# The down products of a step in two parts, with the token group between them

## The chip, the cores and the metric

The kernel runs on one core of a Trainium2 chip. The time is the device time of one execution in microseconds (us); lower is better. Three runs of the kernel before are given, and one more execution was profiled.

## What is computed

Eight sequences of 3008 tokens with 256 channels are Fourier transformed along the sequence, mixed in the frequency domain by a complex 256x256 matrix, soft thresholded, transformed back, and every token then goes through a feed-forward net of 256 -> 2048 -> 256.

```python
def _attn_ref(x, w_r, w_i, b_r, b_i):
    X = np.fft.rfft(x, axis=1)                      # x: (8, 3008, 256)
    Xr, Xi = X.real, X.imag
    Yr = Xr @ w_r - Xi @ w_i + b_r
    Yi = Xr @ w_i + Xi @ w_r + b_i
    Yr = np.sign(Yr) * np.maximum(np.abs(Yr) - 0.01, 0.0)
    Yi = np.sign(Yi) * np.maximum(np.abs(Yi) - 0.01, 0.0)
    return np.fft.irfft(Yr + 1j * Yi, n=3008, axis=1)

def _moe_ref(x, w_in, w_out):                       # x: (24064, 256)
    h = x @ w_in                                    # w_in: (256, 2048)
    g = h * (1.0 / (1.0 + np.exp(-1.702 * h)))
    return g @ w_out                                # w_out: (2048, 256)
```

## The kernel before

3008 is 64 x 47, so the transform is done in two stages, of length 47 and of length 64, each a set of matmuls. All large products are made of three matmuls (`mm3`): weights and data are each split into a rounded high part and a rest, and high x high, high x rest and rest x high are added up in PSUM.

The main loop has 47 x 8 = 376 steps. Tile `k` of the feed-forward net is 512 tokens; step `q` of a tile does 256 of the 2048 hidden channels. A step issues, in the program's order:

- `cur.up(q)`: 12 matmuls of 512 columns (`pa<-th` and `pa<-tl`) into two PSUM banks, each read out by ScalarE with the gated activation (`gb`, L684). From `gb` ScalarE and VectorE make the right factors of the down product: three blocks (`hb`, `lb`) and four sums and differences of blocks (`ht`, `lt`), since the down product is a 2x2 block product with seven multiplications.
- pieces of the spectral work of the next batch (`spectral`): the 64-point stage (`pa<-kr,br`), the mixing (`pa<-wf_h,zz` and `pa<-wf_..,zz`, read out by VectorE as `mv`), the inverse (`pa<-yh,ki`). A list of steps with costs spreads them over the loop.
- `tokens_to(need)`: if the tokens that the coming steps need are not there, the next token group, `tokens(u)`: 376 tokens, about one group in six steps, 64 in all. The first two go another way (`first_tokens`).
- `behind[0].down(behind[1])`: the down products of the step before, 7 right factors x 3 = 21 matmuls of 256 columns into the four output banks `po0` to `po3` (`po<-hb`, `po<-lb`, `po<-ht`, `po<-lt`). `ORDER` gives the seven (left factor, right factor, bank, half): right factors 0, 1, 2, 3, 4, 5, 6, of which 0 to 2 are `hb` and 3 to 6 are `ht`. The fourth is the first that uses `ht`, and it goes to bank 1. Tile 0 is "plain": 4 products of 512 columns.
- After the last step of a tile, `combine()`: two copies of ScalarE (L778, L779) and additions of VectorE and GpSimd read the output banks, and two DMAs on SyncE store the result. `up` of the second step of a tile is queued behind the last down product of the tile before (`after("down")`), and the first down products of the new tile behind that `up` (`after("up")`).

PSUM has eight banks: four for the outputs, and four (`ps_a`, tile name `pa`) that `up`, the spectral stages and the token groups share. A token group writes two of these (64 matmuls `pa<-kz,ur`, the inverse stage of length 47, split into `th` and `tl` by ScalarE and VectorE). In the 40 groups of `u` = 8 to 47 it also does the forward stage of length 47 ("step 47") of a later batch: 8 matmuls `pa<-xt,kp` into two further banks, copied out by ScalarE (`aev`, L495) and stored by SyncE. It also issues the loads of later groups (`ur`, `xt`), all on SyncE's queue.

A *claim* is a matmul of 2 columns (`pa<-wi_h`) into a fresh bank. It takes the wait for that bank, so that the small matmuls behind it have none.

The order of instructions on each engine is planned by the framework's scheduler when the program is built: it goes by the program's order as priority, by what is ready in its own plan, and gives a bank when it is planned free. Where a matmul is not ready, one from further on in the program is issued. Two things tie its hands: inside `with quarters():` TensorE's instructions keep the order in which they are written (others may be issued between them), and `with after(key):` queues the instructions of the block behind the named one on its engine, without waiting for its end.

Of the kernel before, what the change touches and what calls it, by code (L numbers as in the profile page):

```python
# [19 lines left out]
S, N1, N2 = 3008, 64, 47  # L20
# [4 lines left out]
JP = 4 * 2 * N2  # L25
NU = NJ // 4
TOK, HT = 512, 256
NQ = DFF // 256
# [88 lines left out]
def fourier_mix_then_gated_ffn(ctx: ExitStack, tc: tile.TileContext, x, w_r, w_i, b_r, b_i, w_in, w_out, pack, kbs, out):  # L117
    nc = tc.nc
    NB = x.shape[0]
# [13 lines left out]
    def bank():  # L133
        return ps_a.tile([128, 512], F32, name="pa", tag="pa")
# [4 lines left out]
    def buf2(name):  # L139
        return buf([128, 2, D], F32, name, tag="w2", bufs=W2)  # L140

    def after(*keys):
        held = ExitStack()
        for k in keys:
            held.enter_context(tc.issue_after(done_at[k]))
        return held

    def split(hi, lo, src):
        nc.scalar.copy(hi, src)  # L149
        return nc.vector.tensor_tensor(lo, src, hi.bitcast(F32), ALU.subtract)  # L150

    last = [None]

    def mm(ps, w, t, start=True, stop=True):
        last[0] = nc.tensor.matmul(ps, lhsT=w, rhs=t, start=start, stop=stop).ins  # L155

    def mm3(ps, wh, wl, xh, xl, start=True, stop=True):
        mm(ps, wh, xh, start, False)
        mm(ps, wh, xl, False, False)
        mm(ps, wl, xh, False, stop)  # L160
# [16 lines left out]
    parts, done_at = {}, {}  # L177
# [66 lines left out]
    wo_h, wo_l = ([cst.tile([128, NQ // 2, 7, 128], F32R, name=f"wo_{i}a")] * (NQ // 2) for i in range(2))  # L244
# [108 lines left out]
    def quarters():  # L353
        return tc.manual_schedule(engines={mybir.EngineType.PE})

    def claim(ps):

        mm(ps[0:2, 0:2], wi_h[:, 0, 0:2], wi_h[:, 0, 0:2])
# [128 lines left out]
    def dft47_products(ps, t):  # L487
        for c, p in ((1, 1), (0, 0), (0, 1), (1, 0)):
            mm(ps[p][64 * c:64 * c + 64], kp[64 * p:64 * p + 48], t[c][64 * p:64 * p + 48])

    def dft47_out(b, n, ps):
        s1w = s1s[b].rearrange("c f p n j d -> (c f) p n (j d)")
        for p in range(2):
            ev = buf2("aev").rearrange("p j d -> p (j d)")
            nc.scalar.copy(ev, ps[p])  # L495
            nc.sync.dma_start(s1w[:, p, n], ev)
# [101 lines left out]
    def first_tokens(u):  # L598
        t = us.pop(u)
        for c in range(2):  # L600
            ps = bank()
            for j in range(4):
                mm(ps[:, 94 * j:94 * j + 94], t[:96, j, 128 * c:128 * c + 128], kzz)
            for k in range(JP * u // TOK, (JP * (u + 1) - 1) // TOK + 1):
                if k not in ytiles:
                    ytiles[k] = (fbuf([128, 2, TOK], F32R, "th"), fbuf([128, 2, TOK], F32R, "tl"))
                a = JP * u - TOK * k
                n0, n1 = max(0, -a), min(JP, TOK - a)
                split(*(t2[:, c, a + n0:a + n1] for t2 in ytiles[k]), ps[:, n0:n1])
# [11 lines left out]
    def tokens(u):  # L621
        if u < 2:
            return first_tokens(u)
        t = us.pop(u)
        step = steps47.pop(u, None)
        if step:
            b, n, _ = step
            p47 = [bank() for p in range(2)]
        ps = [bank() for p in range(2)]
        pv = [b[:, :JP].rearrange("p (c j n) -> p c j n", c=2, j=4) for b in ps]  # L630
        with quarters():
            for x47 in p47 + ps if step else ps[:1]:
                claim(x47)
            if step:
                dft47_products(p47, step[2])
            for j in range(4):
                for c in range(4):
                    i = 64 * (c % 2)
                    for p in reversed(range(2)):
                        hs = slice(64 * p, 64 * p + 48)  # L640
                        mm(pv[p][i:i + 64, c // 2, j], t[hs, j, 64 * c:64 * c + 64], kz[hs])
        if step:
            dft47_out(b, n, p47)
        for k in range(JP * u // TOK, (JP * (u + 1) - 1) // TOK + 1):
            if k not in ytiles:
                ytiles[k] = (fbuf([128, 2, TOK], F32R, "th"), fbuf([128, 2, TOK], F32R, "tl"))
            th, tl = ytiles[k]
            at = [JP * u + 94 * j - TOK * k for j in range(4)]
            js = [j for j in range(4) if 0 <= at[j] and at[j] + 94 <= TOK]
            for p in range(2):  # L650
                if js:
                    hi, lo = (t[:, :, at[js[0]]:at[js[0]] + 94 * len(js)].rearrange("p c (j n) -> p c j n", j=len(js))[:, :, :, 47 * p:47 * p + 47]
                              for t in (th, tl))
                    split(hi, lo, pv[p][:, :, js[0]:js[0] + len(js)])
                for j in range(4):
                    a = at[j] + 47 * p
                    n0, n1 = max(0, -a), min(47, TOK - a)
                    if j not in js and n0 < n1:
                        split(th[:, :, a + n0:a + n1], tl[:, :, a + n0:a + n1], pv[p][:, :, j, n0:n1])

    def fbuf(shape, dt, name, bufs=2):
        return ff.tile(shape, dt, name=name, tag=name, bufs=bufs)


    ORDER = ((0, 0, 0, 0), (1, 1, 0, 1), (3, 2, 2, 1), (4, 3, 1, 1), (6, 4, 2, 0), (5, 5, 1, 0), (2, 6, 3, 0))
    FIRST, LAST = {0: 0, 2: 2, 1: 3, 3: 6}, {0: 1, 2: 4, 1: 5, 3: 6}

    class Ffn:
        def __init__(self, k):
# [49 lines left out]
            done_at["l"] = split(ht, lt, gt).ins  # L719
            self.g[q] = [(hb[:, i], lb[:, i]) for i in range(3)] + [(ht[:, i], lt[:, i]) for i in range(4)]  # L720

        def down(self, q):
            if q == 0:
                self.acc = [ps_o.tile([128, 2, HT], F32, name=f"po{i}", tag=f"po{i}") for i in range(3 if self.plain else 4)]
            g = self.g.pop(q)
            if self.plain:

                for a, i, bk, first, final in ((0, 0, 0, True, True), (1, 1, 1, True, True), (6, 0, 2, True, False), (2, 1, 2, False, True)):
                    mm3(self.acc[bk], wo_h[q][:, q % 4, a], wo_l[q][:, q % 4, a], *g[i], start=q == 0 and first, stop=q == NQ - 1 and final)
                if q == NQ - 1:  # L730
                    o = [buf2(f"o{i}") for i in range(3)]
                    nc.scalar.copy(o[2], self.acc[0])
                    for e in range(2):
                        nc.vector.tensor_tensor(o[e], self.acc[1 + e], o[2], ALU.add)
                        nc.sync.dma_start(out[self.k, :, e], o[e].rearrange("p h n -> p (h n)"))
                return
            for n, (a, t, bk, h) in enumerate(ORDER):
                mm3(self.acc[bk][:, h], wo_h[q][:, q % 4, a], wo_l[q][:, q % 4, a], *g[t],
                    start=q == 0 and FIRST[bk] == n, stop=q == NQ - 1 and LAST[bk] == n)
            done_at["down"] = last[0]  # L740
            if q == NQ - 1:
                self.combine()
# [52 lines left out]
    done = 0  # L795
# [119 lines left out]
    queue, nextb, behind = [], 1, None  # L915
    for n in range(NT * NQ):
        k, q = divmod(n, NQ)
        if q == 0:
            cur = Ffn(k)
        with after("down") if q == 1 and k > 1 else ExitStack():  # L920
            cur.up(q)
        if n < NQ:
            if n < 7:
                with after("h", "l"):
                    weights(9 + n)
            if n:
                do_early(n)
            if n == 6:
                with after("h", "l"):
                    rounded_parts(pk)  # L930
                ahead = spectral(1, new_s2(1))
                ahead.pop(0)[1]()
            if n == 3:
                pk = packs_in()
        elif not queue and nextb < NB and (nextb < 3 or done >= NU * (nextb - 1)):
            queue = ahead if nextb == 1 else spectral(nextb, new_s2(nextb))
            total, spent, n0 = sum(c for c, _ in queue), 0.0, n
            n1 = NQ * S * nextb // TOK - 16
            nextb += 1
        while queue and spent < total * (n + 1 - n0) / (n1 - n0):  # L940
            c, step = queue.pop(0)
            spent += c
            step()
        need = TOK * (1 + (n + 2) / NQ)
        while queue and need + JP > S * (nextb - 1):
            queue.pop(0)[1]()
        if JP * done < need:
            tokens_to(need)
        if behind is not None:
            with after("up") if q == 1 and k > 1 else ExitStack():  # L950
                behind[0].down(behind[1])
        behind = (cur, q)
    behind[0].down_last(behind[1])

# [34 lines left out]
```

## Time and profile before

| | us |
|---|---|
| median of 3 runs | 2561.44 |
| lowest and highest | 2560.91, 2562.35 |
| profiled execution, first to last instruction | 2562.7 |
| TensorE busy in it | 2542.8 |
| VectorE busy in it | 1931.8 |
| ScalarE busy in it | 1608.2 |

The span of the profiled execution is the time that the profile accounts for; the runs were timed without a profile. The granted clock of TensorE was 0.999 of full speed (2.4 GHz) over the whole run, so its matmuls do not differ in clock.

### The profile page before, as it was taken

How to read it: one execution, taken by the hardware profiler on the slowest of the kernel's cores; microseconds unless marked ns; L12 is line 12 of the kernel's file. 1: busy time of each engine (PE TensorE's matmuls, PEld its weight loads, DVE VectorE, ACT ScalarE, POOL GpSimd, SP SyncE). 2: the span in 40 equal slices, each digit the busy share in tenths (PEclk: the TensorE clock that was granted, in tenths of full speed). 3: DMA queues.
4: the chain of work that ended last, by engine and by line, in shares of the span. 5: the costliest groups of instructions: out<-in, count | busy, mean ns of one | idle time of the engine just before them, and what ended most of it. 6: DMA issues, size and time to landing. Idle time of an engine off the chain costs nothing.

```text
span 2562.7 us, 49527 instructions
## 1 busy us (share of the span) xinstructions
PE 2542.8 (99%) x19979; PEld 2260.5 (88%) x19979; DVE 1931.8 (75%) x3245; ACT 1608.2 (63%) x2627; POOL 50.9 (2%) x65
## 2 busy tenths in 40 slices
PE   9999999999999999999999999999999999999999
PEld 7679999888898888998888988998989999888888
DVE  6788877777777777777777777778767777777776
ACT  4566666666666666666666666666666666665655
POOL 0000000000000000000000000000000000000000
PEclk9999999999999999999999999999999999999999
DMA  8753322333323323233233232332332132200000
GB/s 221 220 161 90 95 87 83 97 90 96 92 72 93 98 89 95 68 96 108 77 95 88 81 106 82 86 91 84 98 100 61 54 89 57 60 30 22 20 13 18
DMA packets 163623, 221.84 MB, mean 87 GB/s; under 512 B 18288, under 2 KB 120912, under 8 KB 163392
## 3 DMA queue, kind: packets, MB, share of 16 engines
q1 hardware_dynamic: 161632, 212.44, 28.6%
q0 software_dynamic: 1760, 6.23, 0.8%
q8 instruction: 157, 2.57, 0.4%
q14 instruction: 74, 0.61, 0.1%
HBM read 117.40 MB, written 101.19 MB: 85 GB/s over the span
## 4 chain that ended last, share of the span: by engine, by line
PE 92%; issue 2%; DVE 2%; ACT 2%; DMA 1%; SPq 0%; POOL 0%; POOLq 0%; DVEq 0%; ACTq 0%
PE pa L155 56%; PE po L155 36%; PE pi L155 0%; DMA s<-iev 0%; ACT gb L684 0%; DMA s<-aev 0%; DVE lb L150 0%; DMA xr<-in_x 0%; DVE lt L150 0%; ACT ht L149 0%; ACT aev L495 0%; PE wm L155 0%; DVE gt L716 0%; PE pt L400 0%; ACT yh L547 0%
## 5 line engine op out<-in xcount | busy, mean ns | idle before, releaser
L684 ACT ACTIVATE gb<-pa 128x512 f32<-128x512 f32 x752 | 447.9, 599 | 399.9 <-PE pa L155 397.0
L150 DVE TENSOR_TENSOR lt<-gt,ht 128x1024 fp32r<-128x1024 f32 x367 | 449.5, 1225 | 245.6 <-ACT ht L149 244.8
L155 PE MATMUL pa<-th,wi_h 128*128 128x512 f32 x1504 | 595.7, 396 | 1.2 <-ACT aev L495 0.7
L155 PE MATMUL pa<-tl,wi_h 128*128 128x512 f32 x1504 | 591.6, 393 | 0.0
L155 PE MATMUL pa<-th,wi_l 128*128 128x512 f32 x1504 | 587.5, 391 | 0.0
L149 ACT CAST ht<-gt 128x1024 fp32r<-128x1024 f32 x367 | 384.5, 1048 | 201.7 <-DVE gt L718 199.2
L716 DVE TENSOR_TENSOR gt<-gb 128x512 f32<-128x512 f32 x367 | 253.1, 690 | 179.5 <-ACT gb L684 172.2
L150 DVE TENSOR_TENSOR lb<-gb,hb 128x768 fp32r<-128x768 f32 x367 | 352.6, 961 | 23.3 <-ACT hb L149 22.9
L155 PEld LDWEIGHTS pa<-th,wi_l 128*128 128x128 f32 x1504 | 283.2, 188 | 58.8
L155 PEld LDWEIGHTS pa<-th,wi_h 128*128 128x128 f32 x1504 | 284.1, 189 | 52.5 <-DVE tl L150 1.9
L155 PEld LDWEIGHTS pa<-tl,wi_h 128*128 128x128 f32 x1504 | 284.4, 189 | 40.4
L149 ACT CAST hb<-gb 128x768 fp32r<-128x768 f32 x367 | 307.0, 837 | 10.3 <-PE po L155 1.1
L155 PE MATMUL po<-lt,wo_0b 128*128 128x256 f32 (+1 forms) x752 | 204.4, 288 | 1.6 <-DVE lt L150 1.1
L155 PE MATMUL po<-lt,wo_0a 128*128 128x256 f32 (+1 forms) x752 | 204.9, 287 | 0.0
L155 PE MATMUL po<-ht,wo_1a 128*128 128x256 f32 (+1 forms) x752 | 203.2, 285 | 0.0
L155 PE MATMUL po<-ht,wo_1b 128*128 128x256 f32 (+1 forms) x752 | 203.0, 286 | 0.0
L155 PE MATMUL pa<-wf_h,zz 128*128 128x256 f32 x1008 | 200.6, 282 | 0.0
L155 PE MATMUL po<-ht,wo_0a 128*128 128x256 f32 (+1 forms) x752 | 177.2, 288 | 1.6 <-DVE o L785 1.5
L155 PE MATMUL po<-ht,wo_0b 128*128 128x256 f32 (+1 forms) x752 | 170.4, 286 | 0.1
L155 PEld LDWEIGHTS pa<-wf_h,zz 128*128 128x128 f32 x1008 | 164.0, 189 | 2.0
L717 DVE TENSOR_TENSOR gt<-gb,gt 128x256 f32<-128x256 f32 x367 | 154.6, 421 | 6.5
L718 DVE TENSOR_TENSOR gt<-gt,gb 128x256 f32<-128x256 f32 x367 | 155.0, 422 | 3.1
(180 smaller groups left out, 4684.1 us busy)
## 6 DMA issues: line engine op xcount, KB each, us to landing
s<-aev SPq DMA_DIRECT2D x112, 256.0 KB, 3.5
s<-iev SPq DMA_DIRECT2D x95, 256.0 KB, 2.4
ur<-s SPq DMA_DIRECT2D x124, 192.0 KB, 3.5
out<-o SPq DMA_DIRECT2D x93, 256.0 KB, 2.1
br<-s SPq DMA_DIRECT2D x168, 128.0 KB, 3.0
yd<-mv SPq DMA_DIRECT2D x168, 128.0 KB, 2.4
yr<-yd SPq DMA_DIRECT2D x84, 256.0 KB, 2.9
xt<-in_x SPq DMA_DIRECT2D x80, 192.0 KB, 3.5
```

Source lines behind the costliest of these rows:

```text
L149: nc.scalar.copy(hi, src)
L150: return nc.vector.tensor_tensor(lo, src, hi.bitcast(F32), ALU.subtract)
L155: last[0] = nc.tensor.matmul(ps, lhsT=w, rhs=t, start=start, stop=stop).ins
L684: done_at["g"] = nc.scalar.activation(o, ps.rearrange("p (h n) -> p h n", h=2), AF.Gelu_apprx_sigmoid).ins
L716: nc.vector.tensor_tensor(gt[:, 0:2], b12, gb[:, 0:3:2], ALU.subtract)
L717: nc.vector.tensor_tensor(gt[:, 2], gb[:, 2], gt[:, 0], ALU.subtract)
L718: nc.vector.tensor_tensor(gt[:, 3], gt[:, 2], gb[:, 1], ALU.subtract)
```

## The change

A step that is going to issue a token group, and whose down products are not those of the plain tile, issues the down products of the first four right factors (12 matmuls, `MID = 4`), then the token group, then the products of the other three (9 matmuls). The last matmul of the first part is remembered as `done_at["mid"]`, and the claims of every later token group are queued behind it. Claims are now made for all banks of a group (four or two; before, a group without step 47 claimed one of its two), and in the opposite order: the two banks of the inverse stage first, then those of step 47. In a step without a token group the down products are issued as before. Where the tile behind is the plain one, its down products now stand ahead of the token group.

```diff
         with quarters():
-            for x47 in p47 + ps if step else ps[:1]:
-                claim(x47)
+            with after("mid") if "mid" in done_at else ExitStack():
+                for x47 in (p47 + ps if step else ps)[::-1]:
+                    claim(x47)
...
+    MID = 4
...
-        def down(self, q):
-            if q == 0:
+        def down(self, q, part=None):
+            if part != 1 and q == 0:
                 self.acc = [...]
-            g = self.g.pop(q)
             if self.plain:
+                if part == 1:
+                    return
+                g = self.g.pop(q)
...
+            g = self.g[q]
             for n, (a, t, bk, h) in enumerate(ORDER):
-                mm3(self.acc[bk][:, h], wo_h[q][:, q % 4, a], wo_l[q][:, q % 4, a], *g[t],
-                    start=q == 0 and FIRST[bk] == n, stop=q == NQ - 1 and LAST[bk] == n)
+                if part is None or part == (n >= MID):
+                    mm3(self.acc[bk][:, h], wo_h[q][:, q % 4, a], wo_l[q][:, q % 4, a], *g[t],
+                        start=q == 0 and FIRST[bk] == n, stop=q == NQ - 1 and LAST[bk] == n)
+            if part == 0:
+                done_at["mid"] = last[0]
+                return
             done_at["down"] = last[0]
...
+        cut = JP * done < min(need, S * NB) and behind is not None and not behind[0].plain
+        if behind is not None:
+            with after("up") if q == 1 and k > 1 else ExitStack():
+                behind[0].down(behind[1], 0 if cut else None)
         if JP * done < need:
             tokens_to(need)
-        if behind is not None:
-            with after("up") if q == 1 and k > 1 else ExitStack():
-                behind[0].down(behind[1])
+        if cut:
+            behind[0].down(behind[1], 1)
         behind = (cur, q)
```

## Rows read from the trace of the kernel before

**Rows 1.** The page: span, then busy time of TensorE and its weight loads.

```profile
span 2562.7 us, 49527 instructions
...
PE 2542.8 (99%) x19979; PEld 2260.5 (88%) x19979; DVE 1931.8 (75%) x3245; ACT 1608.2 (63%) x2627; POOL 50.9 (2%) x65
```

**Rows 2.** Timeline of TensorE, one four-claim group: start us, us, instruction, count.

```profile
1516.99 0.17 PE L155 MATMUL pa<-wi_h 128*2 128x2 f32 x1
...
1518.63 0.17 PE L155 MATMUL pa<-wi_h 128*2 128x2 f32 x1
1518.66 0.36 PE L155 MATMUL po<-lt,wo_0b 128*128 128x256 f32 x1
1518.86 0.28 PE L155 MATMUL po<-ht,wo_1b 128*128 128x256 f32 x1
1518.98 0.28 PE L155 MATMUL po<-lt,wo_0b 128*128 128x256 f32 x1
...
1519.81 0.17 PE L155 MATMUL pa<-wi_h 128*2 128x2 f32 x1
...
1520.82 1.10 PE L155 MATMUL pa<-kz,ur 48*64 48x47 f32 x64
1522.06 0.50 PE L155 MATMUL pa<-th,wi_h 128*128 128x512 f32 x1
```

**Rows 3.** Waits of TensorE: line waited for, us in total, times, longest.

```profile
PE pa L155 <- ACT aev L495: 1.6, 2, 0.9
PE po L155 <- DVE o L785: 1.5, 3, 1.0
```

**Rows 4.** Timeline of TensorE, a group with three claims in a row.

```profile
969.90 0.22 PE L155 MATMUL pa<-wi_h 128*2 128x2 f32 x3
969.98 0.36 PE L155 MATMUL po<-hb,wo_0b 128*128 128x256 f32 x1
970.18 0.28 PE L155 MATMUL po<-lb,wo_0b 128*128 128x256 f32 x1
```

**Rows 5.** Timeline of TensorE, first and last of 102 claims followed by a product.

```profile
120.97 0.17 PE L155 MATMUL pa<-wi_h 128*2 128x2 f32 x1
...
2375.84 0.17 PE L155 MATMUL pa<-wi_h 128*2 128x2 f32 x1
```

**Rows 6.** Timeline of ScalarE in the stretch of rows 2.

```profile
1517.19 0.60 ACT L684 ACTIVATE gb<-pa 128x512 f32<-128x512 f32 x1 [0.38 <-PE pa L155]
...
1521.43 1.07 ACT L495 COPY aev<-pa 128x512 f32<-128x512 f32 x2
```

**Rows 7.** Timelines of TensorE and VectorE, a mix stage ahead of a group.

```profile
769.82 0.28 PE L155 MATMUL pa<-wf_h,zz 128*128 128x256 f32 x1
...
770.83 0.68 DVE L340 TENSOR_TENSOR mv<-pa,mv 128x512 f32<-128x512 f32 x1
```

**Rows 8.** Timeline of TensorE, claim and next product, a whole and two broken groups.

```profile
1949.58 0.17 PE L155 MATMUL pa<-wi_h 128*2 128x2 f32 x1
...
1950.75 0.39 PE L155 MATMUL po<-hb,wo_0a 128*128 128x256 f32 x1
...
2214.67 0.17 PE L155 MATMUL pa<-wi_h 128*2 128x2 f32 x1
...
2216.99 0.38 PE L155 MATMUL po<-hb,wo_0a 128*128 128x256 f32 x1
...
2440.67 0.17 PE L155 MATMUL pa<-wi_h 128*2 128x2 f32 x1
...
2444.04 0.38 PE L155 MATMUL po<-hb,wo_0a 128*128 128x256 f32 x1
```

**Rows 9.** DMA issues on the page: count, KB each, median us to landing.

```profile
ur<-s SPq DMA_DIRECT2D x124, 192.0 KB, 3.5
```

**Rows 10.** Timeline of TensorE, a group in the second step of a tile.

```profile
1205.26 0.19 PE L155 MATMUL pa<-wi_h 128*2 128x2 f32 x2
...
1208.37 0.39 PE L155 MATMUL po<-ht,wo_0a 128*128 128x256 f32 x1 [0.98 <-DVE o L785]
```

## The prediction, made before the changed kernel was built

> **What bounds the kernel now.** I read the page first, then the waits of TensorE, then the timeline of TensorE around the token groups. TensorE works for 2542.8 of the 2562.7 us [rows 1], so nothing that another engine does is worth anything unless TensorE gets shorter: 19.9 us of it are idle, and the rest is a stream of matmuls. The busy figure counts a matmul from its start to a modelled end, and these overlap, so a lost stretch can be hidden in "busy". I therefore went by the distance from one start to the next. A 256-column product of the down stage starts 0.12 us after the one ahead of it (1518.86 to 1518.98) [rows 2]. The waits view gives what TensorE loses to other engines near the edit: 1.6 us for the copies of step 47 (aev), 1.5 us for the last read of an output bank (o, L785) [rows 3]. So the change can only win small things: waits of that size, and the cost of its order inside the stream.
>
> **Where that order costs.** A claim is a 2-column matmul that takes a bank for a token group. Between down products it costs more than itself. At 1518.63 a claim starts, the next product follows at 1518.66, and the product behind that only at 1518.86: 0.20 us instead of 0.12 [rows 2]. So a lone claim costs 0.03 us itself and 0.08 us at the products behind it. Three claims in a row, at 969.90, are over by 969.98, 0.03 us each, and the penalty of 0.08 us (969.98 to 970.18) falls due once [rows 4]. What can be saved is 0.08 us for each claim that no longer stands alone between products. I counted the starts in the trace: 102 of the 194 claims are directly followed by a down product, the first at 120.97, the last at 2375.84 [rows 5].
>
> The Trainium skill would have it otherwise. "TensorE: Matmul & The Clock Gate", section "Step-by-step: what each phase is for", says that weight loads are pulled ahead of matmuls in flight, so that the next weights load while the present matmul runs. By that a claim would cost its own 0.03 us wherever it stands, and gathering claims would give nothing. The gap of 0.20 us speaks against it here, since a 2-column matmul is too short to cover the next load; the second case below shows what the time would be if the page were right.
>
> **The change, part by part.** 62 token groups go through `tokens`; 60 of them come in a step whose `behind` is not the plain tile, and there the new order applies. 40 groups carry step 47 of a later batch and have four claims; 22 had one and now have two.
>
> 1. *Claims pinned behind the fourth factor.* Before, the claims stood ahead of the down products in the program, so each was issued as soon as its bank was planned free, often alone: in the group at 1516.99 one, then after nine products one, after three more one, and the last at 1519.81 after all 21 [rows 2]. Now they come no earlier than behind the twelfth product. All 102 gathered: 102 x 0.08 = 8.2 us. But the last bank may still be planned free only later, and the scheduler may then issue products of the second part between the claims. With one such break in each of the 40 four-claim groups 62 are saved: 5.0 us. I take the middle, 6.6 us. Nothing at all is the lower end, if all four come one by one again.
>
> Are the banks really free behind twelve products? In the group at 1516.99 the twelfth ends about 12 x 0.12 = 1.44 us behind the last up product, at 1518.4; the up stage's last bank is read out at 1517.19 + 0.60 = 1517.79 [rows 6]. The margin is 0.6 us, so no wait. Where a mix stage (wf) stands ahead, the margin is thinner: its last matmul starts at 769.82 and its bank is read until 770.83 + 0.68 = 771.51 [rows 7], 1.7 us against 1.44. That could cost 0.3 us in each of the ten groups that follow such a stage, 3 us; the old order ran more products into that gap, and the planner can do the same with the second part, so I take 0 and keep 3 us for the range.
>
> 2. *One more claim in 22 groups:* 22 x 0.03 = +0.6 us.
>
> 3. *Both banks claimed ahead of the products.* Where only one bank was claimed, four late groups were broken up by the wait for the other. A whole group takes 1.17 us from claim to the next product (1949.58 to 1950.75). The group at 2214.67 takes 2.32 us with six down products in it (0.72): 1.60, so 0.43 too many. The one at 2440.67 takes 3.37 us with twelve (1.44): 1.93, or 0.76 too many [rows 8]. The four are two of each kind: 2.4 us, which I take whole, since both banks are now claimed first. If the claims' wait merely moves ahead of the group, it is 0.
>
> 4. *Second part behind the token products.* Nine products, 1.1 us, can run while ScalarE copies out step 47 (1521.43, two copies in 1.07 us), where before the next up stage started at 1522.06 [rows 2, 6]. Of the waits this can take away, 1.6 and 1.5 us, both together are 3.1 us [rows 3]; some token groups already had down products behind them, and in others the nine will be used up between claims, so I take half, 1.5 us.
>
> 5. *What moves along.* The group's other work (step 47's two copies and two stores, the splits on ScalarE and VectorE, the loads of the next rows) is issued some 1.4 us later, and combine's stores queue on SyncE behind the group's. A row load lands 3.5 us after issue [rows 9] and a group comes only about every six steps, so I cost this at 0. If that cover were gone, a group would wait at most those 3.5 us once. The last down step of a tile now ends behind the tokens, so its combine begins right ahead of the next up stage, without 2 us of token products in between. Such steps without tokens already exist, so I take 1.0 us for the eight groups concerned; none to 8 x 0.98 us (the longest wait for an output bank [rows 10]) are the ends.
>
> Sum: -6.6 + 0.6 - 2.4 - 1.5 + 1.0 = -8.9 us. The profiled execution spans 2562.7 us, 0.05% above the median of the runs, 2561.44. I take the sum off the median: 2552.5 us, -0.35%. A measurement can tell about 0.2% (5.1 us) from no change.
>
> **Rivals.**
>
> *The claims stay scattered, or their place costs nothing.* The pin sets only the earliest moment. If banks are planned free one after another, the claims come one by one between products of the second part, and part 1 falls to about 1 us. For it: the last claim in many old groups came only when all 21 products were out, as at 1519.81 [rows 2], so the plan frees the last bank late. Against it: the first two or three are planned free long before the twelfth product. With part 4 gone too, as the nine products are used up: -1 + 0.6 - 2.4 + 1.0 = -1.8, 2559.6 us. If the place costs nothing, as by the rule above, the sum is 0.6 - 2.4 - 1.5 + 1.0 = -2.3 us, 2559.1 us.
>
> *Slower: the pin waits for an output bank.* Eight groups fall into a tile's second step, where the fourth factor is the first to write output bank 1, which combine must have read. In the group at 1205.26 the old order ran the token products first, and the rest of the down products still waited until 1208.37 for VectorE (L785) [rows 10]. Pinned behind the fourth factor, the tokens could not fill this: up to 3.1 us (1205.26 to 1208.37) in each. All eight cost 25 us: 2561.4 - 8.9 + 25 = 2577 us. From three groups on the gain is gone; from five on it is slower by over 0.2%. Against it: this wait came to 1.5 us in three cases over the whole run [rows 3], and steps without tokens issue the same twelve products in a row. Half of it, four groups, would end at 2565 us.
>
> *A reshuffle.* The whole order is planned anew from the first edited step on, so some of the 19.9 us of idle time [rows 1] will fall elsewhere, with either sign; some 3 us each way go into the range.
>
> **How the numbers follow.** Forecast: 0.60. Claims scattered: 0.22. Place costs nothing: 0.05. Output bank late: 0.13, of which 0.09 over the bound. Nearly all of the forecast lies beyond -5.1 us, and a favourable reshuffle takes a little of the second case there. Faster by over 0.2%: 0.60; within 0.2%: 0.31; slower by over 0.2%: 0.09. The lower end is everything at its best: -8.2 + 0.6 - 2.4 - 3.1 = -13.1, with 3 us of reshuffle 2545.3, say 2546 us. The upper end takes in the scattered claims with the thin margin's 3 us: 2559.6 + 3 = 2562.6, say 2562 us. The forecast's own range is 2546 to 2556 us.
>
> **What would show it.** Right: in the profile after, behind the twelfth product claims in a row (x3 or x4 in one line of the timeline) and no more than one lone claim per group; token products in one piece in the late groups; down products behind the token products; about 40 of the 0.20 us gaps left instead of 102. Wrong: lone claims as before; a wait in front of the claims for VectorE's last reads of the output banks or for mv; TensorE idle for o L785 of over 5 us in all; or the number of 0.20 us gaps going down with no change in time, which would say that I priced them wrongly.

## The result and the profile after

The changed kernel takes 2575.25 us (median of 5 runs, 2574.11 to 2577.51); beside it before takes 2561.44 us. The ratio is 1.0053 [1.0041, 1.0065]: slower by 0.53%, 13.8 us, where 8.9 us less were forecast. The time lies outside the range given (2546 to 2562 us), on the side of the rival "the pin waits for an output bank".

The page of after, span and busy time, answers to [rows 1]:

```profile
span 2575.4 us, 49546 instructions
...
PE 2543.9 (99%) x20001; PEld 2262.7 (88%) x20001; DVE 1933.4 (75%) x3245; ACT 1603.8 (62%) x2627; POOL 51.3 (2%) x65
```

TensorE's busy time grew by 1.1 us, the span by 12.7 us: what came on top is idle time, 31.5 us in place of 19.9. The waits of TensorE in after (line waited for: us in total, times, longest) name the engine behind it, where [rows 3] had 1.6 us for aev and 1.5 us for the output bank. L795 is L786 of before, L794 is L785:

```profile
PE po L155 <- DVE lt L150: 4.1, 9, 0.6
PE po L155 <- DVE lb L150: 2.8, 3, 1.2
...
PE pa L155 <- DVE tl L150: 2.0, 2, 1.8
...
PE po L155 <- DVE o L795: 1.4, 2, 1.0
PE pa L155 <- ACT aev L495: 1.4, 3, 0.6
...
PE po L155 <- DVE o L794: 0.9, 1, 0.9
```

Before, the waits for lt came to 1.1 us in three cases and those for lb to 0.3 us in one. What grew most are waits for VectorE. The same view of before:

```profile
PE po L155 <- DVE lt L150: 1.1, 3, 0.6
```

**What came as forecast.** Timelines of TensorE in after, a four-claim group and a late one (start us, us, instruction, count; in brackets the idle time ahead and what ended it):

```profile
421.15 0.28 PE L155 MATMUL po<-ht,wo_1a 128*128 128x256 f32 x1
421.27 0.24 PE L155 MATMUL pa<-wi_h 128*2 128x2 f32 x4
421.44 1.09 PE L155 MATMUL pa<-xt,kp 48*64 48x512 f32 x8
...
2455.13 0.19 PE L155 MATMUL pa<-wi_h 128*2 128x2 f32 x2
2455.25 1.15 PE L155 MATMUL pa<-kz,ur 48*64 48x47 f32 x64
2456.33 0.38 PE L155 MATMUL po<-lt,wo_0a 128*128 128x256 f32 x1
```

Four claims stand in one line behind the products of the fourth right factor, and the token products follow. I counted in the trace, as for [rows 5]: 216 claims (194 before), and 37 of them are directly followed by a product (102 before). Their price is as reckoned: between products of 256 columns, the product behind such a claim is followed at 0.20 us in all 97 cases of before and all 36 of after. The late group that took 3.37 us with twelve products in it [rows 8] is in one piece and takes 2456.33 - 2455.13 = 1.20 us. All of the last 16 groups do.

**What came on top.** To find it I took the distance of each TensorE instruction's start to the next, less its median in before for the same three instructions in a row (the one ahead, this one and the next, by tile names and shapes), and added up what is over by more than 0.04 us in the main loop: 41.1 us lost in before, 60.9 us in after. The first and second steps of the tiles from tile 2 on, each counted from its first up matmul, hold 12.2 and 28.2 us of these. The growth of 19.8 us lies mainly in these places:

| steps | us more than before |
|---|---|
| the eight second steps with a token group | 5.5 |
| the seven second steps behind a first step with one | 7.6 |
| a third step with a group (1484 us) | 1.1 |
| two first steps without one (2349 and 2483 us) | 2.3 |
| the very last step | 1.7 |

The second step around 625 us shows the first of these. Timelines of TensorE and, below them, VectorE in after:

```profile
621.33 0.40 PE L155 MATMUL po<-ht,wo_0a 128*128 128x256 f32 x2
622.04 0.39 PE L155 MATMUL po<-lt,wo_0a 128*128 128x256 f32 x1 [0.31 <-DVE lt L150]
...
622.62 0.40 PE L155 MATMUL po<-hb,wo_0a 128*128 128x256 f32 x2
623.84 0.38 PE L155 MATMUL po<-lb,wo_0a 128*128 128x256 f32 x1 [0.83 <-DVE lb L150]
...
624.78 0.28 PE L155 MATMUL po<-ht,wo_0a 128*128 128x256 f32 x1
...
625.14 0.24 PE L155 MATMUL pa<-wi_h 128*2 128x2 f32 x4
...
623.71 0.41 DVE L794 TENSOR_TENSOR o<-po,uv 128x256 f32<-128x256 f32 x1
```

Three factors of the step run, then later factors (`ht` at 621.33, behind them a wait of 0.31 us for `lt`), and at 622.62 even products of the next step, which run into a wait of 0.83 us for their own `lb`. The fourth factor starts only at 624.78: it writes output bank 1, which `combine` reads for the last time at 623.71 to 624.12 (L794), and so the plan put it behind the products of the next step. The claims are pinned behind it, at 625.14, so 64 token products and 8 of step 47, which needed none of this, stand and wait. Before, in the group at 1205.26, the token products ran while bank 1 was awaited [rows 10]:

```profile
1206.29 1.10 PE L155 MATMUL pa<-kz,ur 48*64 48x47 f32 x64
```

In other steps it is not the bank. This group of after is in a third step; timeline of TensorE:

```profile
1483.98 0.39 PE L155 MATMUL po<-lt,wo_0a 128*128 128x256 f32 x1 [0.64 <-DVE lt L150]
...
1484.33 0.25 PE L155 MATMUL pa<-wi_h 128*2 128x2 f32 x4
```

`lt` is the last thing that VectorE makes of a step's activations. The fourth factor is the first to need it, and the tokens now stand behind that. This direct case is rare, though: of the six waits for `lt` that after has more than before, two stand right ahead of claims (0.64 us here, 0.45 us in a second step), two are those of the fifth factor in second steps (0.31 us as above, and 0.26 us), and two of 0.64 us are in first steps without a token group, 6.6 us ahead of the next claims. These last can only come from the order around them, which was planned anew; how, stays open.

### The profile page after: what moved, and what is told of

Read it like the earlier page. It is cut to its first block, busy times and chain, and to the rows that moved or that the text cites. A ratio compares the mean times of both kernels' runs of the same rounds, so it can differ in the third digit from the quotient of the medians.

```text
span 2575.4 us, 49546 instructions
## 1 busy us (share of the span) xinstructions
PE 2543.9 (99%) x20001; PEld 2262.7 (88%) x20001; DVE 1933.4 (75%) x3245; ACT 1603.8 (62%) x2627; POOL 51.3 (2%) x65
## 4 chain that ended last, share of the span: by engine, by line
PE 75%; DVE 3%; issue 2%; ACT 2%; DMA 0%; POOL 0%; SPq 0%; POOLq 0%; DVEq 0%; ACTq 0%
PE pa L155 46%; PE po L155 29%; DVE lb L150 1%; DVE lt L150 1%; ACT gb L687 0%; DVE gt L719 0%; ACT ht L149 0%; ACT hb L149 0%; DVE uv L792 0%; ACT yh L547 0%; DVE gt L720 0%; ACT aev L495 0%; DVE tl L150 0%; DVE gt L721 0%; DMA s<-aev 0%
```

## The experiments

All ratios are to the kernel before on the same chip, with 95% intervals; lone claims are those directly followed by a product (before 102, after 37). 0.001 is 2.6 us.

**Where the loss sits: the old order in some steps.** Three kernels cut only where the condition holds (here for the first; `q != 1` and `q != 0` in the other two); elsewhere the group stands ahead of all down products.

```diff
-        cut = JP * done < min(need, S * NB) and behind is not None and not behind[0].plain
-        if behind is not None:
+        late = JP * done < min(need, S * NB) and behind is not None and not behind[0].plain
+        cut = late and q > 1
+        if behind is not None and (cut or not late):
...
+        elif late:
+            with after("up") if q == 1 and k > 1 else ExitStack():
+                behind[0].down(behind[1])
```

Old order in the first two steps of a tile:

> The change as it is, but in the first two steps of a tile (q 0 and 1, 16 of the 62 groups) the token group stands ahead of all 21 down products again. Against the changed kernel's 2575.2 us. Theory A (the loss is at the tile boundary: with the group between the parts, combine of the tile before and the first write of output bank 1 come too late, which the trace after shows as some 16 us more of gaps between TensorE's starts in these steps): these 16 us go, 2559 to 2562 us, slightly faster than or equal to the kernel before. Theory B (right factors late: the products of the fourth factor wait for lt, which the token group used to cover, 3 us in the trace after): 2573 to 2575 us. Theory C (no place in particular, the order was planned anew and fell out badly): anything between 2565 and 2580 us, with the gaps in other places.

Old order in the second step alone:

> The change, but in the second step of a tile (q 1, 8 groups) the token group stands ahead of all down products again. Theory A: the half of the loss that belongs to these groups goes, about 8 of the 16 us: 2567 us, and the waits for VectorE's lb and o in the second steps with a group vanish. Theory B: 2574 to 2575 us. Theory C: no pattern.

Old order in the first step alone:

> The change, but in the first step of a tile (q 0, 8 groups) the token group stands ahead of all down products again, so that combine follows the last down product without a group's products still to come. Theory A: the other half goes, about 8 us: 2567 us. Theory B: 2574 to 2575 us. Theory C: no pattern.

Measured: both 1.0012 [1.0003, 1.0020], the second alone 1.0016 [1.0007, 1.0025], the first alone 1.0031 [1.0019, 1.0042]. Against after's 1.0053 [1.0041, 1.0065] that gives back 10.5, 9.5 and 5.6 us, the last with intervals that just touch; the first kernel, at 2565.69 us, stays above the 2559 to 2562 us expected. The shares of the two steps do not add up (15.1 against 10.5 us). The traces show why they need not: with the old order in the second step, the 5.5 us of the second steps with a group are gone, but so are the 1.7 us of the very last step, which has no group; with the old order in the first step, 3.8 of the 7.6 us behind first-step groups are left, nearly all in tile 26. What an edit gives back lies in part in steps that it does not touch. So most of the loss hangs on the order in these two steps, the larger part, by the middles, on the second. But without it the kernel is still 3.1 us slower than before, with only 50 lone claims: something costs in the other steps too. The waits for lt stood at 3.1 us in the first of the three.

**Bank 1 by itself: fourth and fifth right factor exchanged.** The fifth goes to bank 2, which the third has already opened, so no product ahead of the pin needs bank 1. The sums are the same; the last step's own order, not shown, is changed to match.

```diff
-    ORDER = (..., (4, 3, 1, 1), (6, 4, 2, 0), (5, 5, 1, 0), (2, 6, 3, 0))
-    FIRST, LAST = {0: 0, 2: 2, 1: 3, 3: 6}, {0: 1, 2: 4, 1: 5, 3: 6}
+    ORDER = (..., (6, 4, 2, 0), (4, 3, 1, 1), (5, 5, 1, 0), (2, 6, 3, 0))
+    FIRST, LAST = {0: 0, 2: 2, 1: 4, 3: 6}, {0: 1, 2: 3, 1: 5, 3: 6}
...
```

> The change with the fourth and the fifth right factor exchanged in ORDER (and in the last step): the fourth then still needs ht and lt, but writes output bank 2, which the third has already written; the first write of bank 1 moves behind the cut. The work is the same. The cut behind three factors took away the whole loss; this tells which need of the fourth factor made it. Theory A1 (output bank 1, read late by combine): most of the loss goes here too, 2560 to 2566 us. Theory A2 (ht and lt late): it stays, 2573 to 2577 us, with the waits for lt as in the changed kernel. Both in part: about 2568 us.

Measured: 1.0034 [1.0022, 1.0047], 4.9 us below after by the middles, but the two intervals overlap. The trace is clearer. The same second step, TensorE:

```profile
623.23 0.39 PE L155 MATMUL po<-lt,wo_0a 128*128 128x256 f32 x1 [0.32 <-DVE lt L150]
...
623.57 0.24 PE L155 MATMUL pa<-wi_h 128*2 128x2 f32 x4
```

The claims start 2.13 us behind the first product (621.44) in place of 4.88 us (620.26 to 625.14); the wait for the bank is gone here, and the wait for `lt` is left. In the second steps with a group, 1.6 of the 5.5 us lost are left, so bank 1 costs about 4 us there, much as the times have it. Behind first-step groups 5.9 of the 7.6 us are left, and over the run the waits for lt even grew to 4.6 us. So bank 1 is not the whole of it.

**The fourth factor: the cut behind three.** `hb` and `lb` are all that the first three need, and none of them writes bank 1.

```diff
-    MID = 4
+    MID = 3
```

> The change with the cut behind three right factors in place of four, so that no product that needs ht, lt or output bank 1 stands ahead of the claims. Theory A: the groups in second steps lose their wait for output bank 1 (8 us), those in first steps keep theirs: 2567 us; with B's 3 us on top 2564 us. Theory B alone: 2572 us. Theory C: no pattern.

Measured: 2557.43 us, 0.9983 [0.9974, 0.9992], 4.4 us (0.17%) faster than before and 18 us faster than after, lower than any of the theories put it. 62 lone claims; the stretches lost between starts come to 37.6 us, against 60.9 in after and 41.1 in before. Behind first-step groups, where the expectation kept its loss, 1.0 of the 7.6 us is left. The second step of above in this kernel, TensorE:

```profile
617.12 0.19 PE L155 MATMUL pa<-wi_h 128*2 128x2 f32 x2
617.17 0.48 PE L155 MATMUL po<-ht,wo_0a 128*128 128x256 f32 x2
617.50 0.19 PE L155 MATMUL pa<-wi_h 128*2 128x2 f32 x2
617.62 1.09 PE L155 MATMUL pa<-xt,kp 48*64 48x512 f32 x8
...
619.98 0.38 PE L155 MATMUL po<-ht,wo_0a 128*128 128x256 f32 x1 [0.35 <-DVE o L794]
```

The tokens run from 617.62 on while VectorE reads bank 1, and the fourth factor waits 0.35 us behind them. The waits for lt and for the bank have before's sizes again, 1.1 and 1.5 us in three cases each:

```profile
PE po L155 <- DVE lt L150: 1.1, 3, 0.6
```

The products of one right factor, moved to the other side of the pin, turn the loss into a small gain.

**The fourth factor in the other steps.** The cut behind three, with the old order in the first two steps: it differs from the first kernel of this section in `MID` alone.

> The cut behind three right factors in steps 2 to 7 of a tile, the old order in its first two steps. It differs from the run with the old order in the first two steps and the cut behind four (1.0012 of before) in the fourth right factor of steps 2 to 7 alone, and from the run with the cut behind three everywhere (0.9983) in the first two steps alone. Theory: the fourth factor standing ahead of the tokens is the whole loss, in all steps, through its late operands (ht, lt) as well as through output bank 1; then this run ends at 0.998 to 0.999, some 6 to 8 us under the one with the cut behind four, and TensorE's waits for lt fall from 3.1 us to about 1. Rival: in steps 2 to 7 the fourth factor costs nothing, and its loss is bank 1 in the second step alone; then this run ends at 1.001, as the one with the cut behind four.

Measured: 0.9989 [0.9980, 0.9997] against 1.0012 [1.0003, 1.0020]: put ahead of the pin in the steps q = 2 to 7 of a tile, which do not wait for `combine`, the fourth factor costs 5.9 us. The waits for lt fell from 3.1 us to 1.1. The traces place 1.1 us of it in the group shown next, right ahead of its claims, 2.3 us in the two first steps without a group, and 2.4 us in the second step of tile 26, which has the old order in both kernels. In the same group as above (third step), first the cut behind four, then the cut behind three:

```profile
1478.64 0.39 PE L155 MATMUL po<-lt,wo_0a 128*128 128x256 f32 x1 [0.63 <-DVE lt L150]
...
1478.98 0.24 PE L155 MATMUL pa<-wi_h 128*2 128x2 f32 x4
```

```profile
1476.32 0.22 PE L155 MATMUL pa<-wi_h 128*2 128x2 f32 x3
1476.40 0.36 PE L155 MATMUL po<-hb,wo_0a 128*128 128x256 f32 x1
1476.60 0.17 PE L155 MATMUL pa<-wi_h 128*2 128x2 f32 x1
1476.70 1.09 PE L155 MATMUL pa<-xt,kp 48*64 48x512 f32 x8
```

Four gathered claims were bought with a wait of 0.63 us; three and one come without it. With 10.5 us for the first two steps and 5.9 us for the rest, 16.4 of the 18 us between the two cuts are accounted for by the steps whose order was edited, though not all of it is lost in those steps.

**The cut behind two.**

> The change with the cut behind two right factors. If it matters only that the fourth factor stands behind the claims, this is as fast as the cut behind three, 0.17% below the kernel before, less what is lost where six products (0.7 us) end before the last bank of the up stage is read (0.8 us behind its last product): between 2557 and 2561 us, with more lone claims than the 62 of the cut behind three. If a later cut is better in itself as long as nothing waits, it is slower than the cut behind three by some us.

Measured: `MID = 2` gives 0.9986 [0.9977, 0.9995], with 78 lone claims: it can't be told from three, and the earlier the pin, the fewer claims are gathered.

**The claims' order and the second bank.** Before, with all banks claimed in opposite order and nothing else:

```diff
-            for x47 in p47 + ps if step else ps[:1]:
+            for x47 in (p47 + ps if step else ps)[::-1]:
```

> The kernel before with only the claims edited: all banks of a group claimed, in opposite order, no cut and no pin. My prediction priced it at -2.4 us for the four late groups that were broken up and +0.6 us for 22 claims more: about 2 us below the kernel before, with some 100 lone claims left between products. If the order of the claims gathers them by itself, lone claims fall to about 60 and the time by 3 us more.

Measured: 1.0007 [0.9998, 1.0015], no difference that can be told, where 2 us less were expected; 101 lone claims. The four broken late groups are as broken as before, with both banks claimed at their head; one of them, TensorE:

```profile
2443.32 0.19 PE L155 MATMUL pa<-wi_h 128*2 128x2 f32 x2
2443.45 0.32 PE L155 MATMUL pa<-kz,ur 48*64 48x47 f32 x4
2443.70 0.62 PE L155 MATMUL po<-ht,wo_0a 128*128 128x256 f32 x3
```

Four token products, then down products: the missing bank was not what broke them. And the other way round, the cut behind three with the claims in the old order:

> The cut behind three right factors, with the claims in the old order (the banks of step 47 first, then those of the inverse stage). Theory: the pin gathers the claims and their order among themselves is worth nothing, so the time is that of the cut behind three with claims in opposite order, 0.998 of before, within 0.1%. Rival: the opposite order lets the banks that come free first be taken first; then claims come apart, more than 62 stand alone ahead of a product, and the time goes back towards 1.000.

Measured: 0.9981 [0.9972, 0.9990] against 0.9983 with the opposite order, 62 lone claims in both. The order of the claims is worth nothing that can be told.

**The pin: two parts without it.** The cut behind four, with `after("mid")` left out of the claims:

```diff
-            with after("mid") if "mid" in done_at else ExitStack():
+            with ExitStack():
```

> The change with the down products in two parts, but the claims not queued behind the first part. If the pin is what hurts (TensorE can't fill a wait of the fourth factor with the token group), the group can move ahead again and the loss goes, while claims stand alone again between products: 2560 to 2564 us. If the place of the second part behind the group hurts (combine late), the loss in first steps of a tile stays: 2567 us or more.

Measured: 1.0080 [1.0067, 1.0092], slower than after. TensorE idles no more than before (19.9 us; 43.0 us are lost between starts, against 41.1), and 71 claims are lone; the time goes into groups like this one:

```profile
855.03 0.40 PE L155 MATMUL pa<-kz,ur 48*64 48x47 f32 x16
855.35 0.38 PE L155 MATMUL po<-ht,wo_0a 128*128 128x256 f32 x1
855.67 0.32 PE L155 MATMUL pa<-kz,ur 48*64 48x47 f32 x4
855.91 0.39 PE L155 MATMUL po<-lt,wo_0a 128*128 128x256 f32 x1
...
856.35 0.90 PE L155 MATMUL pa<-kz,ur 48*64 48x47 f32 x44
857.18 0.38 PE L155 MATMUL po<-ht,wo_0a 128*128 128x256 f32 x1
```

The first part stands ahead of the tokens in the program, so its late products are issued as soon as they are ready, into the middle of the token products. From 855.03 to 857.18 are 2.15 us: three products (0.36) and 64 token products that take 1.03 us in one piece in most groups, so 0.76 us are lost. I summed, for the 62 groups, the time from the first claim to the instruction behind the tokens, less 0.12 us for each other matmul of 256 columns in between and 0.23 us for each of 512: 124 us in before, 116 in after, 145 here. So the pin is what keeps the group whole, and what makes it wait.

## Why the prediction was wrong

**The step that failed** is in part 1, "Are the banks really free behind twelve products? [...] so no wait". I checked the banks that the claims take, and assumed that the twelve products themselves run one behind the other from the last up product on. The last three of the twelve, the fourth factor's, need what comes last: `lt`, and in a tile's second step output bank 1. The 12 x 0.12 = 1.44 us reckoned up to the claims were 4.88 us in the second step shown first (620.26 to 625.14); with the cut behind three the first claims stand 1.07 us behind the first product there (616.05 to 617.12). The pin hands the fourth factor's lateness on to the token group, the one piece of work of some 2 us that could have filled it. Part 5 saw that the "2 us of token products in between" are gone behind the last down step of a tile, but priced that at 1.0 us.

**The rival was right in kind and had 0.13.** Both reasons against it were wrong. "This wait came to 1.5 us in three cases" was measured with the tokens filling it, so it was what the cover left over, not what was there. "Steps without tokens issue the same twelve products in a row" does not hold in the trace of before: in the second step around 351 us, TensorE takes matmuls of the coming up stage between them.

```profile
351.29 0.40 PE L155 MATMUL pa<-th,wi_h 128*128 128x512 f32 x1
351.52 0.28 PE L155 MATMUL po<-hb,wo_0a 128*128 128x256 f32 x1
```

In after, the same step is the one behind a token group whose splits came later (`tl` on VectorE at 350.70 in place of 347.53). No up matmul stands in between, and two waits for `combine` do:

```profile
353.12 0.39 PE L155 MATMUL po<-ht,wo_0a 128*128 128x256 f32 x1 [0.38 <-DVE o L795]
...
354.57 0.39 PE L155 MATMUL po<-ht,wo_0a 128*128 128x256 f32 x1 [0.95 <-DVE o L794]
```

The other runs place this in the group of the first step: where that step is cut behind four (old order in the second step alone) the splits start 0.46 us ahead of the first product, no up matmul stands in between and the same two waits are there; where it is not, or is cut behind three, they start 3.1 and 2.5 us ahead, up matmuls (one, in the latter) stand in between, and at most 0.17 us is waited. That it is the banks of the later splits that hold the up stage back was not tried. The rival itself was both too high and too narrow: it had bank 1 in eight groups at up to 3.1 us (25 us). The traces show about 4 us for bank 1 in these groups, 7.6 us in the second steps behind first-step groups, which the rival did not have, and the runs 5.9 us in the order of the other steps, without bank 1. The reshuffle, the third rival, had 3 us each way; the 1.7 us of the last step and the 2.3 us of the two first steps are of its kind.

The terms of the sum, by what was measured:

- Part 1, gathered claims: 65 fewer lone claims, x 0.08 = -5.2 us, inside the stated -8.2 to -5.0. That the place of a claim costs, and not only its number, fits the rows above: in the cut behind three the product at 1476.40 and the claim at 1476.60 are 0.20 us apart again. No run here had the place alone changed. The Trainium skill ("TensorE: Matmul & The Clock Gate", "Step-by-step: what each phase is for") says that the next weights load while the present matmul runs; what the prediction drew from it, that a claim costs only itself wherever it stands, is not borne out by that gap.
- Part 2, 22 claims more: as forecast, +0.7 us by count at 0.03 us each (22 x 0.03 = 0.66; the prediction has 0.6).
- Part 3, broken late groups: the 2.4 us came, but by the pin, which starts these groups later; claiming both banks alone left all four broken, and with the cut behind two, two of them are broken again. What breaks them in before stays open.
- Part 4, the second part behind the tokens: of the 1.5 us little came. The waits for aev went from 1.6 to 1.4 us, those for `o` L785 and L786 from 1.5 us to 2.3 us (0.9 and 1.4).
- Not in the sum: 19.8 us of new lost stretches. -5.2 + 0.7 - 2.4 + 19.8 = 12.9 us, against 12.7 in the spans; the counts overlap, and the lost stretches move by some us with how the kinds are told apart, so that the sum comes out this close is luck.

With the fourth factor taken out the same terms are 40 x -0.08 + 0.7 - 2.4 - 3.5 = -8.4 us, where the runs of the cut behind three show -4.4 [-6.7, -2.0] and their profile -7.3. So the forecast's mechanism existed at about half its forecast size, and the step named above cost 18 us. The cut behind three, with the claims in either order, is the fastest version found, by its interval faster than both kernels, though by less than 0.2% than before.

## What to carry to other kernels

When work is pinned behind an instruction, list every operand of that instruction and when it is ready, before looking at what the pinned work itself needs: the pin inherits the latest of them. A short wait in the waits view can be what is left after something filled it; before moving the filler, read from a timeline how long the wait would be without it. Where a cut is to be made, put it where operand classes change (here behind the last product that needs only `hb` and `lb`), not at the middle of the count. And where the whole order is planned anew, look for what an edit gives and takes in steps that it does not touch, too.

## What the runs showed of the hardware

After two short waits TensorE ran at half clock for a while. Timeline of TensorE in after, a second step in which `combine` itself was late (its first addition on VectorE waited 2.69 us for a DMA, and `tl` and `yh` came behind it), then the windows (us, busy time of TensorE, its weight loads, VectorE, ScalarE and GpSimd, granted clock, DMA share, GB/s):

```profile
1533.59 0.47 PE L155 MATMUL pa<-yh,ki__1662 128*128 128x512 f32 x1 [1.84 <-DVE tl L150]
...
1535.41 1.22 PE L155 MATMUL pa<-yh,ki__1662 128*128 128x512 f32 x2 [1.00 <-DVE yh L548]
1536.42 0.42 PE L155 MATMUL po<-ht,wo_0a 128*128 128x256 f32 x1
1536.64 0.42 PE L155 MATMUL po<-lt,wo_0a 128*128 128x256 f32 x1
```

```profile
1532.00:1534.30 2.30, 0.71 (x4) 0.60 (x4) 2.21 (x6) 0.34 (x1) 0.19 (x1) 1.00 0.36 114
1534.30:1536.40 2.10, 1.10 (x3) 0.84 (x3) 2.07 (x6) 0.00 (x0) 0.00 (x0) 0.63 0.28 103
1536.40:1538.10 1.70, 1.70 (x9) 1.67 (x8) 1.70 (x4) 1.43 (x4) 0.00 (x0) 0.50 0.50 190
```

TensorE waited 1.84 and 1.00 us with four matmuls in between; the granted clock is still 1.00 over the first wait, 0.63 in the 2.1 us that hold the second, and 0.50 (1.2 GHz) in the following 1.7 us, in which TensorE did not wait at all. There the products start 0.21 us apart in place of 0.12: eight of them, 0.7 us on top of the waits. The Trainium skill has this in general ("TensorE: Matmul & The Clock Gate", "HAM oscillation — how this bites in real kernels": work behind a wait can start at the lower clock); the trace agrees, with waits of 1.84 and 1.00 us. So a wait can cost more than its own length, in a kernel that has TensorE busy 99% of the time. The wait for the DMA itself is not new: in before the same addition waited 3.06 us, but TensorE then waited only 0.35, 0.16 and 0.18 us, with other matmuls in between. The cut behind three holds 1.00 from 1526 to 1538 us; with the fourth and fifth factor exchanged the clock was 0.50 from 1532.9 to 1539.7 us. Before has such a stretch too, so not all its matmuls ran at one clock: 0.50 from 116.7 to 120.0 us, behind a wait of 1.52 us for a DMA.
